# Attention's output transposed by DMA and normalised on GpSimd, in a kernel that runs top-k attention and a Fourier mix

## The chip, the cores and the metric

The kernel runs on one core of one Trainium2 chip. A core has a matrix engine (TensorE, PE in the profile, its weight loads PEld), a vector engine (VectorE, DVE), a scalar engine (ScalarE, ACT), a general engine (GpSimd, POOL) and a synchronisation engine (SyncE, SP) that here issues nearly all DMA transfers. Each engine works through its own instructions in order and waits on semaphores for the others. The metric is the device time of one execution in microseconds (us).

## The reference, cut to what matters

```python
# attention: batch 8, heads 8, tokens 576, head size 64
scores = scale * q @ k.T
kth = np.partition(scores, -32, axis=-1)[..., -32:-31]
scores = np.where(scores >= kth, scores, -1e9)
attn = softmax(scores)                       # sum + 1e-9
x = (attn @ v) laid out as [batch, token, 8 * 64]

# Fourier mix: d_model 512, hidden 2048
mixed = real(fft(fft(x, axis=1), axis=2))
u = x + mixed
un = (u - mean(u)) / sqrt(var(u) + 1e-6)
out = u + relu(un @ w_ch1) @ w_ch2
```

All of it is in 32-bit floats. The inputs are q, k and v of shape [8, 8, 576, 64] and the two weight matrices.

## The kernel before

**Tiles and steps.** Two heads make a pair, so there are 32 pairs, four for each batch. The 576 queries of a pair are cut into tiles: eight tiles of 128 queries of one head, and one tile with the 64 remaining queries of both heads. That is nine tiles a pair (IN_PAIR, PER_PAIR), 36 a batch, 288 in all. One main loop (L1485) runs over steps i, one step for each tile, and goes on behind the last tile until all planned work is done. A step issues work of several tiles: the scores of tile i+3 on PE, the top-32 search of tile i on DVE (four MAX8 and three MATCH_REPLACE8 over 576 scores, `top_ops`, L422 and L424), the bounds of tile i on POOL (`bounds`, L431), the mask of tile i-1 (ACT L443, POOL L446) and its exponentials (ACT L454).

**From the exponentials to the attention's output.** In pairs 4 to 30 without pair 7 (`by_dma`, L435) the exponentials reach TensorE over DRAM. One step after the exponentials, `plane` has ACT copy their 16-bit low and high halves into two planes (L467), and SP write them to DRAM (L480, L483). One step later, `turn` has SP bring them back with a DMA transpose (L501) into PT, with keys on the partitions. In the other pairs TensorE transposes them (`transposes`). A pair's queries form two chunks: chunk 0 has 320 queries and chunk 1 has 256 (CW). `attend` multiplies PT by v for one chunk, 20 matmuls in the profile (L559), into the PSUM tile o, which has one buffer (ps_o). `chunk_at` says in which step this happens: the fourth after the chunk's last tile in the pairs with DMA, as the last of the step's matmuls.

**From the output to tokens.** `attended` (L568) follows at once in the same step: ACT copies o to SBUF as xT (L573), copies two denominators (L578) and adds 1e-9 to the denominators (L585); DVE takes the reciprocals one step later (L586). Then the chunk is put in the list pending, for the next step or later. `to_tokens` (L589) takes it from there, one chunk a step at most: TensorE transposes xT in three or two pieces into PSUM (tpx, L599), and DVE multiplies by the reciprocals into x (L603, L610). In batch 1 ACT does this multiplication instead, in pieces of one head (L622). x holds all tokens of a batch and has two buffers. A chunk of batch b therefore waits in pending until the output of batch b-2 has been put out (`written`).

**The Fourier mix.** When a batch's four pairs are in x, its later stages are planned in steps counted from T0 (L1377), which is end + 5 for batches 2 to 6, where end is the step of the batch's last tile. The stages are: folds on POOL (`fold_tails`, `fold_ops`), the token DFT (`dft_tokens`, PE L750), the channel DFT (`dft_channels`, PE L807 and L811), statistics on DVE, an inverse square root on DVE and POOL, and transposes to channels first (PE L876). Then the MLP of the batch is cut into units (`mlp_units`) that enter a queue: 32 units with the hidden layer (PE L961, ACT L965), then units with the second layer (PE L988, L1027, and for one chunk a form with seven half-size products, PE L1158, with sums on POOL L1103 and L1130 and with parts of w2 that SP loads, L904). `level` (L1458) sets how much PE work a step should have, so that the queue is empty when the next batch's units arrive; `fixed_cost` (L1447) is its estimate of what a step has in any case. Units are put between the fixed pieces of a step. Work behind the last tile, the stages and MLP of the last batch, has no attention beside it.

**Order around the change.** In each step the order of issue is: `turn`, mask and `plane`; the scores of a new tile and their ACT copies; the list planned for "act" and the list out_next; then the other pieces with units between them; then `attend` and `attended`; the loads of q, k and v (SP, L240 to L288); the DVE search; the list planned for "pool0"; the bounds; and the lists "dve", "pool", "load" and "load2".

Of the kernel before, what the change touches and what calls it, by code (L numbers as in the profile page):

```python
# [73 lines left out]
def kernel(  # L74
# [359 lines left out]

    def by_dma(i):  # L435

        pair = i // PER_PAIR
        return NPB <= pair < NPAIR - 1 and pair != 2 * NPB - 1
# [129 lines left out]
    def attended(pair, ch, late):  # L568

        o, w = o_of.pop((pair, ch)), CW[ch]  # L570
        PT.pop((pair, ch))
        xT = attp.tile([P, CW[0]], F32, name=f"xT_{pair}_{ch}", tag="xT", bufs=4)
        nc.scalar.copy(out=xT[:, 0:w], in_=o[:, 0:w])  # L573
        xT_of[pair, ch] = xT
        den = den_t[pair % 3]
        if ch == 0:
            for h in range(2):
                nc.scalar.copy(  # L578
                    out=den[TH * h:TH * (h + 1), 5:6],
                    in_=den[TAIL + TH * h:TAIL + TH * (h + 1), 4:5],  # L580
                )
        c0, n = (0, 6) if ch == 0 else (6, 4)
        rd = small.tile([P, 6], F32, name=f"rd_{pair}_{ch}", tag="rd", bufs=6)

        nc.scalar.activation(out=rd[:, 0:n], in_=den[:, c0:c0 + n], func=AF.Copy, bias=1e-9)  # L585
        late.append(lambda: nc.vector.reciprocal(out=rd[:, 0:n], in_=rd[:, 0:n]))  # L586
        rd_of[pair, ch] = rd

    def to_tokens(pair, ch, at_once=True):  # L589
# [5 lines left out]
        xT, rd = xT_of.pop((pair, ch)), rd_of.pop((pair, ch))  # L595
        shape, name = [P, 4, P], f"tpx_{pair}_{ch}"
# [3 lines left out]
        cols = slice(P * hp, P * (hp + 1))  # L600
# [772 lines left out]
    for b in range(B):  # L1373
# [3 lines left out]
        T0 = end + (2 if first else 3 if soon else 4 if last else 5)  # L1377
# [69 lines left out]
    def fixed_cost(i):  # L1447
# [5 lines left out]
        t += 0.0 if ch is None else (CW[ch] / 115.0 + 0.14 * len(CHUNKS[ch]))  # L1453
# [31 lines left out]
    while i < N + 5 or plan or queue or sums:  # L1485
# [117 lines left out]
        for where in ("pool", "pool2", "load", "load2"):  # L1603
            run(i, where)
# [40 lines left out]
```

## Time and profile before

| | |
|---|---|
| time, three runs | median 1886.04 us (1885.32 to 1888.74) |
| the profiled execution's own time | 1888.63 us |
| its span, first to last instruction | 1886.8 us |
| granted TensorE clock, mean | 0.954 of full speed |
| busy, share of the span | PE 1724.3 us (91%), DVE 1582.2 (84%), ACT 1295.8 (69%), POOL 912.1 (48%) |
| DMA | 249 MB, 51% of the 16 DMA engines' time |

The profile is of one execution. Engines' busy times leave out waiting and the issuing of DMAs. A line number such as L573 is a line of the kernel before. A group of instructions is written as line, engine, operation, output<-inputs with shapes, and count, and then busy time, the mean duration of one in nanoseconds, and the idle time of the engine just before them with what ended it. The matmuls overlap in the pipeline, so that the mean duration of one is longer than the distance from one to the next. A wait "ACT xT L573 <- PE o L559" says that ACT stood idle before the instruction of line 573 until the matmul of line 559 was done. SPq lines are instructions of SyncE's queue.

### The profile page before, as it was taken

Reading aid. Unit: us, or ns where it says so; the run is one execution under the profiler, and the core shown is the slowest. Engines: PE = TensorE matmul, PEld = TensorE weight load, DVE = VectorE, ACT = ScalarE, POOL = GpSimd, SP = SyncE. Lnnn points to the kernel's source line nnn. Section 1 sums busy time; section 2 is a strip of 40 time slices with the busy share of each in tenths; the row PEclk is TensorE's granted clock in tenths of the full one; section 3 lists DMA queues with packets and bytes.
Section 4 is the critical chain, followed back from the end, with each engine's and each line's share of the span. In section 5 each row is a group of like instructions: output and inputs, shape, how many; then the busy total and the mean of one; then the engine's idle time right before and its main releaser. Section 6 shows DMA issues by size and latency. Waiting matters only on the chain.

```text
span 1886.8 us, 26907 instructions
## 1 busy us (share of the span) xinstructions
PE 1724.3 (91%) x8134; PEld 1089.6 (58%) x8134; DVE 1582.2 (84%) x3301; ACT 1295.8 (69%) x3104; POOL 912.1 (48%) x1278
## 2 busy tenths in 40 slices
PE   6667699889899999999999999999999999999999
PEld 3344365355456654566456665566556655667677
DVE  7999999799899999997998898999999899862110
ACT  6878658577787777776777677777787678652100
POOL 4768644454745366354643465355544464341012
PEclk8778899899899999999999999999999999999999
DMA  5333026661557755575465845586467655440132
GB/s 166 103 97 108 20 63 160 166 156 32 137 149 193 186 130 137 140 202 140 122 157 136 225 121 128 142 220 156 120 160 179 179 132 144 120 117 6 51 110 72
DMA packets 516576, 249.16 MB, mean 132 GB/s; under 512 B 398288, under 2 KB 506448, under 8 KB 516432
## 3 DMA queue, kind: packets, MB, share of 16 engines
q1 hardware_dynamic: 515664, 247.23, 50.6%
q8 instruction: 65, 1.06, 0.2%
q14 instruction: 79, 0.65, 0.1%
q10 hardware_dynamic: 768, 0.21, 0.0%
HBM read 93.63 MB, written 84.74 MB: 95 GB/s over the span
## 4 chain that ended last, share of the span: by engine, by line
PE 63%; DVE 12%; ACT 10%; POOL 6%; DMA 4%; issue 3%; SPq 2%; POOLq 0%; DVEq 0%; ACTq 0%
PE hp L961 23%; PE cp L988 8%; PE o L559 7%; DVE m L422 5%; PE sp L398 5%; DVE wk L424 5%; PE cw L1158 3%; PE yp L750 3%; PE cv L1158 3%; PE cp L1027 2%; POOL wk L446 2%; ACT wk L443 2%; ACT wk L467 2%; PE sp_t L368 2%; PE mp L811 1%
## 5 line engine op out<-in xcount | busy, mean ns | idle before, releaser
L446 POOL TENSOR_TENSOR wk<-S,wk 128x576 f32<-128x576 f32 x288 | 408.6, 1419 | 572.2 <-ACT wk L443 570.0
L422 DVE MAX8 m<-wk 128x8 f32<-128x576 f32 x864 | 626.4, 749 | 6.0
L961 PE MATMUL hp<-unT,w 128*128 128x256 f32 (+1 forms) x2048 | 535.5, 412 | 3.6 <-ACT hT L965 2.8
L961 PEld LDWEIGHTS hp<-unT,w 128*128 128x128 f32 x2048 | 378.5, 191 | 134.5 <-issue 30.1
L424 DVE MATCH_REPLACE8 wk<-m,wk 128x576 f32<-128x576 f32 x576 | 427.4, 742 | 0.0
L467 ACT COPY wk<-S 128x576 uint16<-128x576 uint16 x468 | 288.7, 666 | 0.1
L443 ACT ACTIVATE wk<-S,nt 128x576 f32<-128x576 f32 x288 | 222.2, 772 | 73.0 <-POOL nt L431 72.1
L988 PE MATMUL cp<-w,hT 128*128 128x512 f32 x512 | 244.6, 614 | 0.0
L422 DVE MAX8 m<-S 128x8 f32<-128x576 f32 x288 | 213.9, 743 | 31.9 <-ACT S L372 31.8
L559 PE MATMUL o<-PT,v 128*64 128x256 f32 (+3 forms) x1440 | 205.1, 429 | 19.3 <-DMA PT<-planes 15.4
L424 DVE MATCH_REPLACE8 wk<-m,S 128x576 f32<-128x576 f32 x288 | 213.5, 741 | 0.0
L965 ACT ACTIVATE hT<-hp 128x320 f32<-128x320 f32 (+1 forms) x256 | 103.6, 409 | 155.3 <-PE hp L961 154.5
L454 ACT ACTIVATE S<-wk,nt 128x576 f32<-128x576 f32 x234 | 182.6, 781 | 39.9 <-POOL wk L446 38.9
L398 PE MATMUL sp<-kT,qT 64*128 64x512 f32 (+1 forms) x528 | 183.1, 693 | 12.2 <-ACT means L1346 5.1
L559 PEld LDWEIGHTS o<-PT,v 128*64 128x64 f32 x1440 | 118.0, 158 | 105.0 <-issue 35.5
L988 PEld LDWEIGHTS cp<-w,hT 128*128 128x128 f32 x512 | 93.4, 195 | 109.5 <-issue 107.7
L401 ACT COPY S<-sp 128x512 f32<-128x512 f32 (+1 forms) x264 | 141.6, 586 | 18.5 <-PE sp L398 17.6
L1103 POOL TENSOR_TENSOR hT<-hT 128x512 f32<-128x512 f32 x64 | 81.3, 1274 | 99.0 <-ACT hT L965 86.2
L368 PEld LDWEIGHTS sp_t<-kt,qT 128*128 128x128 f32 x320 | 55.7, 198 | 100.6 <-ACT S L390 44.2
L368 PE MATMUL sp_t<-kt,qT 128*128 128x128 f32 x320 | 72.1, 308 | 45.0 <-ACT S L390 29.8
L431 POOL TENSOR_TENSOR nt<-m,cc 128x2 f32<-128x2 f32 x288 | 58.9, 205 | 111.9 <-DVE m L422 108.9
L1158 PE MATMUL cw<-w,hT 128*128 128x256 f32 x448 | 105.7, 383 | 0.7 <-issue 0.6
(160 smaller groups left out, 2137.9 us busy)
## 6 DMA issues: line engine op xcount, KB each, us to landing
planes<-wk SPq DMA_DIRECT2D x208, 288.0 KB, 2.7
w<-w_parts SPq DMA_DIRECT2D x82, 512.0 KB, 4.7
space<-in_moe_w_ch_dram SPq DMA_DIRECT2D x32, 512.0 KB, 3.7
nat<-in_q_dram SPq DMA_DIRECT2D x128, 64.0 KB, 2.4
v<-in_v_dram SPq DMA_DIRECT2D x64, 128.0 KB, 3.0
out_dram<-x SPq DMA_DIRECT2D x32, 256.0 KB, 2.6
nat<-in_k_dram SPq DMA_DIRECT2D x62, 128.0 KB, 2.9
planes<-wk SPq DMA_DIRECT2D x52, 144.0 KB, 2.6
```

Source lines behind the costliest of these rows:

```text
L368: nc.tensor.matmul(sp[:, 0:P], lhsT=qT[:, q_end - P:q_end], rhs=kt_t, start=True, stop=True)
L398: nc.tensor.matmul(sp[r], lhsT=qT[hd, q_cols], rhs=kT[hd, :], start=True, stop=True)
L422: ops.append(lambda src=src, m8=m8: nc.vector.max(out=m8, in_=src))
L424: ops.append(lambda src=src, m8=m8: nc.vector.match_replace(w, m8, src, NEG))
L443: nc.scalar.activation(out=w, in_=Ssb[i], func=AF.Relu, scale=-FAR, bias=Nt[i][:, 1:2])
L446: nc.gpsimd.tensor_tensor(out=w, in0=Ssb[i], in1=w, op=ALU.subtract)
L454: nc.scalar.activation(out=Ssb[i] if by_dma(i) else w, in_=w, func=AF.Exp, bias=Nt.pop(i)[:, 0:1], accum_out=den_t[pair % 3][:, c:c + 1],)
L467: nc.scalar.copy(out=words[:, half, :], in_=src[:, half, :])
L559: nc.tensor.matmul(o[D * e:D * (e + 1), c0:c1], lhsT=vv[:, c, e, :], rhs=pt[:, NF if c == NF else (NF + 1) * e + c, c0:c1], start=(c == 0) ...
L961: nc.tensor.matmul(hp[:, 0:w], lhsT=w1[:, dt, P * it:P * (it + 1)], rhs=unT[:, dt, 0:w], start=(dt == 0), stop=(dt == NDT - 1),)
L988: nc.tensor.matmul(cp, lhsT=hT[:, it, P * n:P * (n + 1)], rhs=w2[:, it, :], start=(it == 0), stop=(it == NIT - 1),)
L1158: nc.tensor.matmul(dst, lhsT=h()[a][:, kc, :], rhs=rhs_of(kc), start=start and kc == 0, stop=kc == NK - 1, skip_group_check=True,)
```

## The change

In the pairs 4 to 30 without 7 (now `pair_by_dma`) a chunk's output goes to x without TensorE and DVE:

- ACT copies o twice, as 16-bit low and high halves, into two planes in SBUF, instead of once in 32 bits.
- SP writes the planes to DRAM (one write for chunk 1, two for chunk 0), and `to_tokens` has SP bring them back with DMA transposes straight into x (one for chunk 1, two for chunk 0), at the end of the step in which the chunk is taken from pending.
- POOL multiplies x in place by the reciprocals two steps later, in the list "pool0", ahead of the step's bounds (one instruction for chunk 1, two for chunk 0).
- `attended` is put in out_next for all of these chunks but the last of each batch: its ACT copies then stand in the next step, behind the copies of the scores. The chunk can be taken from pending from the step after that on, also in a step that has a chunk's `attend`.
- T0 of batches 2 to 6 is two steps later, end + 7, and the loop's end and `fixed_cost` follow.

```diff
         o, w = o_of.pop((pair, ch)), CW[ch]
         PT.pop((pair, ch))
-        xT = attp.tile([P, CW[0]], F32, name=f"xT_{pair}_{ch}", tag="xT", bufs=4)
-        nc.scalar.copy(out=xT[:, 0:w], in_=o[:, 0:w])
-        xT_of[pair, ch] = xT
+        if pair_by_dma(pair):
+            words = attp.tile([P, 2, CW[0]], U16, name=f"ow_{pair}_{ch}", tag="xT", bufs=4)
+            src = o[:, 0:w].bitcast(U16).rearrange("p (s h) -> p h s", h=2)
+            for half in range(2):
+                nc.scalar.copy(out=words[:, half, 0:w], in_=src[:, half, :])
+            to = xT_of[pair, ch] = dramp.tile(
+                [P, 2, CW[0]], U16, name=f"oplanes_{pair}_{ch}", tag="oplanes", bufs=6
+            )
+            nc.sync.dma_start(out=to[:, :, TAIL:], in_=words[:, :, 0:2 * P])
+            if ch == 0:
+                nc.sync.dma_start(out=to[:, :, 0:TAIL], in_=words[:, :, 2 * P:])
+        else:
+            xT = attp.tile([P, CW[0]], F32, name=f"xT_{pair}_{ch}", tag="xT", bufs=4)
+            nc.scalar.copy(out=xT[:, 0:w], in_=o[:, 0:w])
+            xT_of[pair, ch] = xT
...
         xT, rd = xT_of.pop((pair, ch)), rd_of.pop((pair, ch))
+        cols = slice(P * hp, P * (hp + 1))
+        if pair_by_dma(pair):
+            rows = xT.rearrange("p h s -> (p h) s")
+            nc.sync.dma_start_transpose(
+                out=x[:, 2 * ch:2 * ch + 2, cols].bitcast(U16), in_=rows[:, TAIL:]
+            )
+            if ch == 0:
+                nc.sync.dma_start_transpose(out=x[:, 4:5, cols].bitcast(U16), in_=rows[:, 0:P])
+
+            def normalise_in_place():
+                for t0, nt, n, r in ((2 * ch, 2, 0, P), (4, 1, 4, TAIL))[:2 - ch]:
+                    xs = x[0:r, t0:t0 + nt, cols].rearrange("p t (e d) -> p t e d", e=2)
+                    by = rd[0:r, n:n + 2 * nt].rearrange("p (t e) -> p t e", e=2)
+                    nc.gpsimd.tensor_tensor(
+                        out=xs, in0=xs, in1=by.to_broadcast([r, nt, 2, D]), op=ALU.mult
+                    )
+
+            at(now[0] + 2, "pool0", normalise_in_place)
+            return 0.0
...
-        T0 = end + (2 if first else 3 if soon else 4 if last else 5)
+        T0 = end + (2 if first else 3 if soon else 4 if last else 7)
...
         if pending and pending[0][0] <= i and (
-            i < 2 * PER_BATCH + 4 or chunk_at(i)[0] is None
+            i < 2 * PER_BATCH + 4 or chunk_at(i)[0] is None or pair_by_dma(pending[0][1])
         ):
             _, pp, pc = pending[0]
             if pp // NPB < 2 or pp // NPB - 2 in written:
                 pending.pop(0)
-                tok.append(lambda: to_tokens(pp, pc, not short))
+                if not pair_by_dma(pp):
+                    tok.append(lambda: to_tokens(pp, pc, not short))
+                else:
+                    at(i, "turn", lambda: to_tokens(pp, pc))
...
             cost += attend(pair, ch)
-            attended(pair, ch, late_next)
-            pending.append((i + 1, pair, ch))
+            if pair_by_dma(pair) and (pair % NPB, ch) != (NPB - 1, 1):
+                out_next.append(lambda pair=pair, ch=ch: attended(pair, ch, late_next))
+                pending.append((i + 2, pair, ch))
+            else:
+                attended(pair, ch, late_next)
+                pending.append((i + 1, pair, ch))
...
-        for where in ("pool", "pool2", "load", "load2"):
+        for where in ("pool", "pool2", "load", "load2", "turn"):
             run(i, where)
```

More of the change, by code (lines that the diff above doesn't have):

```diff
@@ L433, in bounds, with pair_by_dma @@
             )
+    def pair_by_dma(pair):
+        return NPB <= pair < NPAIR - 1 and pair != 2 * NPB - 1
     def by_dma(i):
-        pair = i // PER_PAIR
-        return NPB <= pair < NPAIR - 1 and pair != 2 * NPB - 1
+        return pair_by_dma(i // PER_PAIR)
     def mask(i, then=None):
@@ L599, in to_tokens @@
             nc.tensor.transpose(tp[0:ROWS[t], n, :], xT[:, P * n:P * n + ROWS[t]], ident)
-        cols = slice(P * hp, P * (hp + 1))
         def normalise():
@@ L1452, in fixed_cost @@
         ch = chunk_at(i)[1] if i > PER_BATCH + 3 else {4: 0, 8: 1}.get((i - 3) % PER_PAIR)
-        t += 0.0 if ch is None else (CW[ch] / 115.0 + 0.14 * len(CHUNKS[ch]))
+        t += 0.0 if ch is None else (
+            CW[ch] / 115.0 + (0.0 if by_dma(i - 4) else 0.14 * len(CHUNKS[ch]))
+        )
         if i < N and i % PER_PAIR in (0, 5):
@@ L1484 @@
     i, carry = 0, 0.0
-    while i < N + 5 or plan or queue or sums:
+    while i < N + 7 or plan or queue or sums:
         now[0] = i
```

## The prediction

> **What bounds the kernel now.** I read the busy shares first, by stage. Each line is a stretch of the run: us, then busy time and instruction count of PE, PEld, DVE, ACT and POOL, the granted TensorE clock, the DMA share and GB/s.
>
> ```profile
> 450.00:860.00 410.00, 377.09 (x1759) 230.12 (x1757) 379.82 (x789) 307.33 (x728) 207.09 (x307) 0.95 0.61 153
> 860.00:1640.00 780.00, 756.32 (x3638) 473.88 (x3637) 717.93 (x1494) 594.74 (x1420) 393.41 (x591) 0.98 0.60 151
> 1640.00:1887.00 247.00, 241.92 (x1129) 177.80 (x1127) 70.98 (x155) 60.41 (x147) 56.17 (x80) 1.00 0.24 74
> ```
>
> From 860 us on TensorE sets the pace (97% busy, VectorE 92%); behind 1640 it works almost alone. Between 450 and 860 the two are level (92% and 93%), so whichever is late holds the other. The next view is the chain that ended last, in order of time; a line is start, duration, what.
>
> ```profile
> 1000.05 0.22 PE tpx L599 x2
> 1000.27 2.16 PE hp L961 x8
> ...
> 1004.80 0.33 PE tpx L599 x3
> ...
> 1052.89 2.48 DMA planes<-wk
> ...
> 1055.43 5.20 DMA PT<-planes
> ```
>
> The reader is to see two things. The output's transposes (tpx) lie on the chain, but each costs only 0.11 us there, since matmuls overlap. And the chain does pass through the DMA route of the probabilities, one write and one transpose, 7.7 us in a row. Then the waits: who waited for whom, total us, times, longest; the last two lines are SyncE's own waits.
>
> ```profile
> POOL wk L446 <- ACT wk L443: 570.0, 247, 14.7
> ...
> ACT xT L573 <- PE o L559: 86.3, 38, 11.8
> ...
> DVE x L603 <- PE tpx L599: 47.3, 18, 6.6
> ...
> PE sp_t L368 <- ACT S L390: 29.8, 21, 3.6
> ...
> PE o L559 <- DMA PT<-planes: 15.4, 6, 7.4
> ```
> ```profile
> SPq L480 <- ACT wk L467: 374.7, 133, 16.9
> SPq L501 <- DMA planes<-wk: 202.9, 107, 4.1
> ```
>
> GpSimd has hundreds of idle microseconds. ScalarE stands still for o at 38 of 64 chunks, and TensorE for probabilities only at 6. Last, the prices: groups by shape (count, busy us, mean ns, idle before), and the duration of SyncE's transposes (min/median/max ns).
>
> ```profile
> L603 DVE TENSOR_TENSOR x<-tpx,rd 128x256 f32<-128x256 f32 x57 | 24.0, 421 | 53.9 <-PE tpx L599 47.3 <-DMA nat<-in_q_dram 3.0 <-issue 1.4
> L610 DVE TENSOR_TENSOR x<-tpx,rd 64x128 f32<-64x128 f32 x28 | 7.6, 273 | 0.0
> L573 ACT COPY xT<-o 128x320 f32<-128x320 f32 x32 | 13.7, 427 | 51.1 <-PE o L559 51.1
> L573 ACT COPY xT<-o 128x256 f32<-128x256 f32 x32 | 11.9, 371 | 35.4 <-PE o L559 35.2
> L918 POOL TENSOR_TENSOR w_t<-w 128x256 f32<-128x256 f32 x16 | 11.7, 731 | 34.8 <-DMA w_parts<-w_t 34.8
> ```
> ```profile
> L501 SPq DMA_TRANSPOSE PT<-planes x130: 1293/2504/7872, 254.6 to 1651.1; - x130
> ```
>
> **The change, part by part.** The sum is made against the profiled execution, 1888.6 us (span 1886.8). That is 2.6 above the median of 1886.0, which I take off at the end. Affected are pairs 4 to 30 without 7: 26 pairs, 52 chunks.
>
> *TensorE's transposes go.* Five a pair, 130 of 160. At the 0.11 us of the chain that is 0.55 a pair, 14.3 in all (the 280 ns of their row would make 36, but that row counts the overlapped latency). Pairs 16 to 30 lie in the stretch that TensorE bounds: 15 x 0.55 = 8.2, all of it on the path. The other 11 pairs hold 6.0; VectorE is level there, so I take half. -11.2, ends -14.3 and -4. What is late next is VectorE, 5 points behind.
>
> *VectorE's normalise goes.* 22 pairs (4 to 6 do it on ScalarE) by 2 x 421 + 273 ns = 1.1 us, 24.5 in all, and waits of 47.3 for tpx. From 860 on VectorE has cover from TensorE, so there I count nothing; without that cover the 15 pairs are worth 16.7. For pairs 8 to 15 the work is 8.9 and the waits in that window 9.7. Ends 0 and -18.6, I take a third: -6.
>
> *ScalarE's copies.* Two 16-bit copies per chunk take the place of one of 32 bits. No row shows a 16-bit copy out of PSUM. Below, it costs what the 32-bit copy of as many elements does (427 and 371): +0.8 us a pair, +21. Above, 666 ns each, the row of the 576-element 16-bit copies (L467): 2.66 for 0.80, +48. I take the lower, which has the same element count and source. Pairs 4 to 6 lose ten ScalarE multiplies of about 0.32 each (L622), -9.6. Net +11 of busy time on an engine that is 69% busy: +2 on the path, ends -9.6 and +38.
>
> *The wait for o goes.* L573 stood at the end of the step of its matmuls, and behind it in ScalarE's queue were the denominators, the next step's mask and planes, and the scores' copies. Now 47 of the 52 stand behind the scores' copies of the next step, which come after o on TensorE anyway. ScalarE still waits for TensorE there, but mask and planes are done by then. TensorE itself is hurt by a late ScalarE where sp_t waits for a free bank: 29.8 on L390 above, and 14.8 on L401 in the same view. I take a sixth of the 44.6, since most of it belongs to steps without a chunk: -7. Ends -30 (two thirds of it), and +10 if the copies, now ahead of exp and of the q and k copies, delay those by 0.4 us at 26 places.
>
> *The later stages of batches 2 to 6 move two steps back.* With T0 move the folds (GpSimd), both DFT stages, their ScalarE copies, statistics and rsqrt, the MLP's units, and what these put on SyncE's queue: the loads of w2's parts and the output stores. One batch has 535.5 + 244.6 + 64.7 + 209.5 (L961, L988, L1027, L1158) = 1054/8 = 132 us of MLP on TensorE, 3.7 a step of 36. Two steps' worth, 7.3, moves out of the time that VectorE shares into the time behind the last scores. Batch 1's MLP is thinned over two steps more, which gives a part back. +5, ends 0 and +11.6 (two whole steps; 15 pairs of nine steps in 780 us make 52 a pair, 5.8 a step).
>
> *GpSimd's normalise comes.* Per pair two of 128x256 and one of 64x128, by L918 and the 465 ns of the 128x128 rows: 1.9 us, 50 in all. It stands two steps behind the transpose's issue, before the bounds (L431); behind those wait ScalarE's mask, then L446, then exp. Cover: 570 us of idle time before L446, and the two vector instructions, 1.5 us, that follow a tile's last MAX8 in its step. +1, ends 0 and +10; a gain is excluded, since it only adds.
>
> [...]
>
> *SyncE and the DMAs.* 78 writes and 78 transposes more, in a queue of 650 to 800 instructions. A write's issue took 0.56 (L480). No row has a transpose this small: 131 KB for two blocks of tokens, 66 KB for the tails, against 590 KB in 2.50 us. By size 0.56 and 0.28 us of issue; above, 1.29 each, the shortest seen. So 2.8 to 5.6 us of SyncE in a pair's 52. The write waits for ScalarE's copies; behind it stand the loads of k, v and q. The transposes wait for that write, once a batch also for the output store of batch b-2, and behind them stands the next PT<-planes, for which TensorE's o matmuls wait. SyncE's 375 us of waiting for ScalarE are the cover. +5, ends 0 and +30.
>
> Sum: -11.2 - 6 + 2 - 7 + 5 + 1 + 5 = -11.2. 1888.6 - 11.2 = 1877.4, less 2.6: 1875.
>
> **The rivals.**
> *Slower: the probabilities queue behind the output.* Place: SyncE, where the x transposes stand just ahead of the next PT<-planes. For it: the chain runs through that route already (1052.89 to 1060.6), and SyncE took up to 7.9 us for one transpose. Against it: 46 of 52 chunks had no such wait. Price: 0.6 to 2.6 us at each chunk that has no slack; at 14 of 52 and 2 us it is 28 in place of my 5: 1898. It decides from about 8 chunks on (16 us in place of 5 cancels the gain).
> *Given back at the end.* The two steps cost their full 11.6, and VectorE's part hides behind ScalarE and GpSimd between 290 and 860: -11.2 + 2 - 7 + 11.6 + 1 + 5 = +1.4, 1887. For it: TensorE has 242 of 247 us behind 1640, so nothing there absorbs more. Against it: batch 1 gets the two steps.
> *More than that.* ScalarE's 86 us of waiting for o is what makes sp_t late: -30 in place of -7, 1852. For it: 35 sp_t waits in the two rows, 1.3 us each. Against it: L390's step comes once a pair, not next to a chunk's.
> That the change does not do what it says is excluded by its order: 130 fewer transposes, 78 more on SyncE.
>
> **How the numbers follow.** About 0.2% (3.8 us) is what this measurement can tell from no change. Forecast 0.46, slower rival 0.28, given back 0.15, more 0.11. Faster: 0.40 of the forecast's, all of the third and a little of the second, 0.53. Slower: 0.26 of the first rival, 0.07 of the second, 0.03 of the forecast's, 0.36. The rest, 0.11, is within. Range: from the third rival, 1852, to the first with the shift's upper end, 1898 + 6, and 3 of ScalarE: 1907. The forecast's own range is 1865 to 1884.
>
> **What would show it.** Right: tpx rows 30 in place of 160, ScalarE's wait for o under 20 us, VectorE's wait for tpx under 15; TensorE above 96% from 860 on; sp_t's waits for L390 below 24. SyncE's x transposes at 0.3 to 1.3 us. Wrong: o's wait for PT<-planes above 30 us, bounds or L446 waiting for x transposes, last scores later than before, or more than 255 us behind them.

## The result and the profile after

The change makes the kernel slower: median 1900.4 us (1897.6 to 1903.2, four runs) against 1886.9, a ratio of 1.0068 with a 95% interval of 1.0053 to 1.0084, or +13.5 us. The prediction was 1875, a gain; its stated range, 1852 to 1907, holds the measured time near its slow end.

The busy shares by stage of the changed kernel (columns as before the change):

```profile
450.00:860.00 410.00, 370.86 (x1722) 224.98 (x1718) 381.50 (x783) 315.00 (x751) 217.69 (x321) 0.96 0.68 167
860.00:1640.00 780.00, 735.28 (x3485) 458.06 (x3483) 694.98 (x1421) 590.35 (x1413) 407.71 (x622) 0.98 0.65 160
1640.00:1902.00 262.00, 255.11 (x1184) 186.08 (x1182) 70.50 (x155) 65.57 (x163) 62.44 (x90) 1.00 0.26 76
```

TensorE, which set the pace from 860 to 1640 us, now stands idle for 780 - 735.3 = 44.7 us there; before it was 780 - 756.3 = 23.7. Its clock in that stretch is the same. Behind 1640 it has 13 us more to do.

The waits say for what it stands (who, for whom: total us, times, longest):

```profile
DVE m L422 <- ACT S L372: 81.6, 31, 7.8
...
PE sp_t L368 <- ACT S L401: 22.8, 15, 6.3
...
PE o L561 <- DMA PT<-planes: 19.1, 11, 6.1
...
PE cw L1190 <- DMA w<-w_parts: 15.9, 6, 5.1
PE sp_t L368 <- ACT S L390: 15.1, 15, 2.7
...
PE cp L1059 <- DMA w<-w_parts: 13.1, 6, 3.2
...
POOL x L623 <- DMA x<-oplanes: 12.8, 12, 2.1
...
DVE x L635 <- PE tpx L632: 6.5, 3, 3.2
...
ACT ow L578 <- PE o L561: 2.1, 2, 1.3
```

What the change was to remove is gone: ScalarE's wait for o fell from 86.3 to 2.1 (and 9.3 where the old path stays), VectorE's wait for tpx from 47.3 to 6.5. VectorE's search now waits longer for the copied scores (81.6 for 31.8). What is new stands in a place that the prediction did not price: TensorE waits 15.9 + 13.1 = 29.0 us for `w<-w_parts`, the loads of w2's parts between the seven products of the later stages. In the kernel before, the only such row of TensorE's matmuls was this:

```profile
PE cp L1027 <- DMA w<-w_parts: 6.0, 2, 5.5
```

From 860 us on, in the stretch where TensorE is idle for 21.0 us more, the kernel before has no such row, and the changed kernel has these two, 17.5 us together:

```profile
PE cw L1190 <- DMA w<-w_parts: 10.5, 3, 3.6
...
PE cp L1059 <- DMA w<-w_parts: 7.0, 3, 2.7
```

One of these waits in the chain of the changed kernel that ended last (start, us, what):

```profile
1035.71 2.49 SPq L503
...
1038.31 0.57 SPq L485
...
1038.93 0.60 SPq L485
...
1039.62 4.42 DMA w<-w_parts
1044.05 0.14 issue
1044.18 5.39 PE cw L1190 x16
```

The load stands in SyncE's queue behind a transpose of the probabilities (2.49) and two writes of their planes (0.57 and 0.60); ahead of these SyncE issued one of the change's own transposes (L613, 1.21 us from 1034.46). The load then takes 4.42 us, and TensorE starts 0.14 us after it has landed. TensorE had stood still for 3.3 us.

Where the 14.5 us between the two profiled spans lie can be read from the start of the bounds of a pair's first tile. Up to pair 16 the changed kernel gains 13.9 (861.3 to 847.4 us). From pair 16 to pair 31 it takes 796.4 in place of 778.9, +17.5. From pair 31 to the end it takes 257.5 in place of 246.7, +10.8. Such a split compares single executions. It also compares schedules: an edit that moves stages changes which units the planner puts into which step.

### The profile page after: what moved, and what is told of

It reads as the page before. It is cut to its first block, busy times and chain, and to the rows that moved or that the text cites. A ratio compares the mean times of both kernels' runs of the same rounds, so it can differ in the third digit from the quotient of the medians.

```text
span 1901.3 us, 26874 instructions
## 1 busy us (share of the span) xinstructions
PE 1705.1 (90%) x8004; PEld 1073.9 (56%) x8004; DVE 1564.7 (82%) x3232; ACT 1304.7 (69%) x3126; POOL 951.0 (50%) x1356
## 4 chain that ended last, share of the span: by engine, by line
PE 55%; DVE 13%; POOL 9%; DMA 8%; ACT 8%; SPq 3%; issue 3%; POOLq 0%; DVEq 0%; ACTq 0%
PE hp L993 18%; PE cp L1020 8%; PE o L561 6%; DVE m L422 6%; DVE wk L424 5%; PE sp L398 4%; PE cw L1190 4%; PE cv L1190 3%; DMA w<-w_parts 3%; POOL wk L448 3%; PE yp L782 3%; PE cp L1059 3%; DMA PT<-planes 2%; ACT wk L445 2%; DMA planes<-wk 2%
## 5 line engine op out<-in xcount | busy, mean ns | idle before, releaser
L422 DVE MAX8 m<-S 128x8 f32<-128x576 f32 x288 | 214.6, 745 | 84.5 <-ACT S L372 81.6
L445 ACT ACTIVATE wk<-S,nt 128x576 f32<-128x576 f32 x288 | 222.4, 772 | 77.2 <-POOL nt L431 76.8
L1020 PE MATMUL cp<-w,hT 128*128 128x512 f32 x512 | 238.0, 604 | 0.0
L561 PE MATMUL o<-PT,v 128*64 128x256 f32 (+3 forms) x1440 | 201.9, 425 | 23.9 <-DMA PT<-planes 19.1
L398 PE MATMUL sp<-kT,qT 64*128 64x512 f32 (+1 forms) x528 | 172.2, 674 | 15.8 <-ACT means L1378 5.1
L1190 PE MATMUL cw<-w,hT 128*128 128x256 f32 x448 | 112.9, 401 | 18.0 <-DMA w<-w_parts 15.9
L1190 PEld LDWEIGHTS cw<-w,hT 128*128 128x128 f32 x448 | 86.8, 200 | 36.4 <-issue 20.7
```

The source lines that it names most:

```text
L398: nc.tensor.matmul(sp[r], lhsT=qT[hd, q_cols], rhs=kT[hd, :], start=True, stop=True)
L422: ops.append(lambda src=src, m8=m8: nc.vector.max(out=m8, in_=src))
L445: nc.scalar.activation(out=w, in_=Ssb[i], func=AF.Relu, scale=-FAR, bias=Nt[i][:, 1:2])
L561: nc.tensor.matmul(o[D * e:D * (e + 1), c0:c1], lhsT=vv[:, c, e, :], rhs=pt[:, NF if c == NF else (NF + 1) * e + c, c0:c1], start=(c == 0) ...
L1020: nc.tensor.matmul(cp, lhsT=hT[:, it, P * n:P * (n + 1)], rhs=w2[:, it, :], start=(it == 0), stop=(it == NIT - 1),)
L1190: nc.tensor.matmul(dst, lhsT=h()[a][:, kc, :], rhs=rhs_of(kc), start=start and kc == 0, stop=kc == NK - 1, skip_group_check=True,)
```

## The experiments

Medians of each kernel beside runs of the kernel before on the same chip; the ratio is to those, with its 95% interval.

### The two parts that need no DMA

The shift of the later stages alone, in the kernel before:

```diff
-        T0 = end + (2 if first else 3 if soon else 4 if last else 5)
+        T0 = end + (2 if first else 3 if soon else 4 if last else 7)
```

> The kernel before, with only the later stages of batches 2 to 6 two steps back (end + 7). Theory S (the new writes and transposes fill SyncE's queue, and TensorE waits behind them for parts of w2 and for probabilities): about what the prediction had for this part, +5, 1887 to 1893, and no wait of TensorE for w<-w_parts above 2 us in all from 860 us on. Rival T (the two steps back are the loss, because the MLP's loads now meet the attention's in the wrong steps): 1898 or more, with such waits.

Measured 1901.3, ratio 1.0071 (1.0043 to 1.0099). The shift alone costs about as much as the whole change, 14.4 us by the medians and 8 to 19 by the interval, and it brings the waits that rival T named. Its profiled execution is the fastest of its four and 8.9 us longer than the one before: up to pair 16 it gains 9.2, from there to pair 31 it loses 9.9, and behind pair 31's start 8.2. TensorE's matmuls wait 15.3 us for w2's parts in place of 6.0.

The later place of ScalarE's copies alone, in the kernel before:

```diff
-            attended(pair, ch, late_next)
-            pending.append((i + 1, pair, ch))
+            dma_pair = NPB <= pair < NPAIR - 1 and pair != 2 * NPB - 1
+            if dma_pair and (pair % NPB, ch) != (NPB - 1, 1):
+                out_next.append(lambda pair=pair, ch=ch: attended(pair, ch, late_next))
+                pending.append((i + 2, pair, ch))
+            else:
+                attended(pair, ch, late_next)
+                pending.append((i + 1, pair, ch))
```

> The kernel before, with only ScalarE's copies of o (still one of 32 bits) moved into the next step behind the scores' copies. Theory S with the prediction's sizes: 7 less, 1876 to 1883, ScalarE's wait for o under 15 us in place of 86. Rival: the 15 us by which the changed kernel is ahead at pair 18 come from VectorE and TensorE, freed of the transposes, and this part alone gives nothing, 1884 to 1889.

Measured 1885.0, ratio 0.9993 (0.9974 to 1.0011): no difference. ScalarE's wait for o, 86.3 us before, is 10.8 in this kernel, and the time is the same. By the pairs' starts its profile gains 15.7 us up to pair 16, as much as the changed kernel, and loses 8.9 and 2.8 behind it. So this early gain also comes where TensorE's transposes and VectorE's normalise stay.

### The output's DMAs

The changed kernel without them; x is multiplied from a constant table, so the output's way to x is left out. Then the same with the 78 writes put back.

```diff
-            nc.sync.dma_start(out=to[:, :, TAIL:], in_=words[:, :, 0:2 * P])
...
-            nc.sync.dma_start_transpose(
...
-                        out=xs, in0=xs, in1=by.to_broadcast([r, nt, 2, D]), op=ALU.mult
+                        out=xs, in0=fd[0:r, 0:nt, :].rearrange("p t (e d) -> p t e d", e=2), in1=by.to_broadcast([r, nt, 2, D]), op=ALU.mult
```

> The changed kernel without the writes and transposes of the output: x is multiplied from a table instead, so the later stages work on other numbers; all else stays, the two steps back, the 16-bit copies and GpSimd's multiply. Theory S: the loss goes, 1868 to 1880. Rivals (the two steps back, ScalarE's second copy, GpSimd's multiply ahead of the bounds): 1893 to 1900.

> The same, but the 78 writes of the output to DRAM stay and only the 78 transposes are left out. SyncE's time for them is 49 us of writes and 103 of transposes. Theory S, by SyncE's time: about a third of what the run without both gains is lost again, 1875 to 1886. If the waits of the transposes count (for the write's landing, for x), and not the time they take, this run is as fast as the one without both.

Measured 1872.0 (0.992, 0.9895 to 0.9946) without any, and 1890.2 (1.0013, 0.9995 to 1.0031) with the writes. The first lies in the range of theory S, with both steps of the shift still in place. The second lies above its range: in this schedule the writes make 18 us and the transposes 10 more. TensorE's waits for w2's parts are 20.5, 30.4 and 29.0 us in the three kernels, those for the probabilities (PE and PEld) 15.5, 20.2 and 27.9.

Three ways to make the same DMAs cheaper followed: the writes at the end of the step, the writes issued by ScalarE, and the transposes behind the probabilities' transpose of the next step.

```diff
+            at(now[0], "turn", write)
```

> The changed kernel with the output's writes put at the end of their step in SyncE's order, behind the loads of w2's parts, of k, q and v, in place of right behind ScalarE's copies. The same 78 writes and transposes. Theory wait (the writes cost 18 us because SyncE stands still for ScalarE's copies in the middle of the step, and the loads behind it with it): 10 to 18 less than the changed kernel, 1882 to 1890. Rival time (what counts is the 0.57 us that each write takes of SyncE): unchanged, 1897 to 1903.

```diff
-            nc.sync.dma_start(out=to[:, :, TAIL:], in_=words[:, :, 0:2 * P])
+            nc.scalar.dma_start(out=to[:, :, TAIL:], in_=words[:, :, 0:2 * P])
```

> The changed kernel with the output's writes issued by ScalarE behind its own copies, in place of SyncE. Theory wait and theory time both: SyncE is rid of them, and 12 to 18 us go, 1882 to 1890, if ScalarE's 78 issues of about 0.5 us are hidden. If the DMA engines' load, not SyncE, is what counts: unchanged, 1897 to 1903.

```diff
-            at(now[0] + 2, "pool0", normalise_in_place)
+            at(now[0] + 1, "pool0", normalise_in_place)
...
-                    at(i, "turn", lambda: to_tokens(pp, pc))
+                    at(i + 1, "turned", lambda pp=pp, pc=pc: to_tokens(pp, pc))
...
+        run(i, "turned")
```

> The changed kernel with the output's transposes one place later in SyncE's order, behind the next step's transpose of probabilities in place of ahead of it. Theory order (the loss by the transposes, 10 us, is the probabilities' queueing behind them): 5 to 10 less, 1890 to 1896, and TensorE's wait for PT<-planes back to about 16 us. Theory time: unchanged, 1897 to 1903.

Measured 1905.0 (1.0103, 1.0077 to 1.013), 1914.4 (1.0146, 1.0127 to 1.0165) and 1917.5 (1.0173, 1.014 to 1.0205). None is faster than the changed kernel (the first is 5 us slower, little more than the noise), so the gains that the theories of waiting, time and order expected did not come. The last two edits bring a cost of their own, so they do not exclude that SyncE's time or the order has a part. In the second, ScalarE stands still for 53.0 us at its 78 issues: 36.6 ahead of the denominators' copies and 16.4 ahead of the addition of 1e-9, two waits that the changed kernel does not have. In the third, GpSimd's multiply stays in its step with its input a step later, and its wait grew to this (the changed kernel: 12.8). TensorE's wait for the probabilities grew there too, from 19.1 to 24.5, though their transposes now went first:

```profile
POOL x L623 <- DMA x<-oplanes: 39.2, 25, 4.8
```

The writes with their bytes cut to a sixteenth (no transposes, x from the constant table):

```diff
-            nc.sync.dma_start(out=to[:, :, TAIL:], in_=words[:, :, 0:2 * P])
+            nc.sync.dma_start(out=to[0:8, :, TAIL:], in_=words[0:8, :, 0:2 * P])
```

> The kernel with the 78 writes and without the transposes (x is multiplied from a constant table, the output's way to x is left out), with each write cut from 128 partitions to 8: the same number of issues on SyncE, in the same places with the same waits, a sixteenth of the bytes and descriptors. With full writes it took 1890.2, without any 1872.0. Theory 'bytes' (the DMA engines' load delays the probabilities and the weights): 1873 to 1877. Theory 'issue' (SyncE's instructions and what they wait for cost, whatever they carry): 1887 to 1892. Between the two, both take part, in that proportion.

Measured 1893.4 (1.0024, 1.0011 to 1.0038): as slow as with all bytes. The bytes are not the cause of the writes' 18 us.

### The shift, again

One step in place of two, with GpSimd's multiply one step behind the transposes:

```diff
-            at(now[0] + 2, "pool0", normalise_in_place)
+            at(now[0] + 1, "pool0", normalise_in_place)
...
-        T0 = end + (2 if first else 3 if soon else 4 if last else 7)
+        T0 = end + (2 if first else 3 if soon else 4 if last else 6)
```

> The changed kernel with GpSimd's multiply one step behind the transposes in place of two, which lets the later stages of batches 2 to 6 begin at end + 6, one step back in place of two. Theory shift (two steps back cost 8 to 10 us of TensorE's work behind the last scores): half of it goes, 3 to 6 less, 1894 to 1898, the stretch behind pair 31's first bounds 252 to 254 us in place of 257.5. If GpSimd now waits for the transposes and holds back the bounds: 1900 to 1910.

Measured 1932.0 (1.0243, 1.0218 to 1.0269), 32 us slower than the changed kernel and outside both ranges. The multiply now waits, and behind it wait the bounds, then ScalarE's mask (76.8 in the changed kernel). The later stages moved too, so how much of the 32 is the multiply's is not shown:

```profile
ACT wk L445 <- POOL nt L431: 116.4, 68, 6.9
POOL x L623 <- DMA x<-oplanes: 58.0, 26, 7.7
```

No output DMAs and no shift (x from the constant table, T0 at end + 5, the multiply at once):

```diff
-            at(now[0] + 2, "pool0", normalise_in_place)
+            normalise_in_place()
...
-        T0 = end + (2 if first else 3 if soon else 4 if last else 7)
+        T0 = end + (2 if first else 3 if soon else 4 if last else 5)
```

> The kernel without the output's DMAs (x is multiplied from a constant table, so that the output's way to x is left out and the result is not the reference's), but with the later stages of batches 2 to 6 where they stood before the change (five steps behind the batch's end), and the multiply at once. Theory A (the parts add): the shift alone cost 14.4 us, the DMAs 28.4, so what the change removes, net of what it adds on ScalarE and GpSimd, is worth 1900.4 - 28.4 - 14.4 - 1886.9 = -29; expected 1857.6, within 5. Theory B (the shift costs only in a schedule that is already tight, and is hidden where the output's work is gone): as with the shift, 1872, within 4; the removed work is then worth only 15.

Measured 1900.8 (1.0063, 1.0045 to 1.0081). Both theories miss, by 43 and 29 us: taking the shift out of the kernel of 1872 made it 29 slower, where putting the shift into the kernel before made that 14 slower. Prices for the parts do not add. The multiply's new place shows no cost in the waits: GpSimd waits 1.9 us before it, and the mask's wait for the bounds is 75.9 (75.5 in the kernel of 1872). Here too TensorE waits for w2's parts (20.8 us), now in three waits of 4.4 to 5.3 us between 1050 and 1480 us. Around one of them the windows of 4 us of that kernel show what such a wait brings besides itself (the number behind POOL's is the granted clock):

```profile
1260.00:1264.00 4.00, 0.00 (x0) 0.00 (x0) 3.96 (x9) 2.55 (x5) 1.56 (x2) 0.91 1.04 294
1264.00:1268.00 4.00, 3.70 (x11) 1.68 (x13) 0.77 (x2) 0.00 (x0) 0.00 (x0) 0.50 0.82 224
1268.00:1272.00 4.00, 4.00 (x19) 2.02 (x16) 0.00 (x0) 0.00 (x0) 0.00 (x0) 0.74 0.82 190
```

TensorE runs no matmul for 4 us, and then at half its clock for over 4 us. The half clock makes this kernel lose more than its waits say. Over the two halves of the stretch from 860 us, first this kernel, then the one of 1872:

```profile
860.00:1250.00 390.00, 373.28 (x1767) 234.00 (x1766) 353.16 (x725) 302.51 (x724) 211.72 (x321) 0.97 0.59 150
1250.00:1640.00 390.00, 368.41 (x1712) 227.23 (x1711) 339.36 (x695) 288.15 (x688) 195.10 (x305) 0.96 0.58 146
```
```profile
860.00:1250.00 390.00, 374.67 (x1776) 236.35 (x1775) 356.27 (x729) 303.36 (x728) 212.30 (x321) 0.98 0.61 155
1250.00:1640.00 390.00, 373.29 (x1799) 233.45 (x1798) 354.14 (x724) 296.77 (x711) 204.12 (x314) 1.00 0.59 147
```

The lost clock, 0.01 and 0.04 of 390 us, is worth about 4 and 16 us by estimate.

The last pair of each batch by TensorE and VectorE as before, so that the shift can be undone in a kernel with the whole result; and the same with one write a chunk:

```diff
+    def out_by_dma(pair):
+        return pair_by_dma(pair) and pair % NPB != NPB - 1
...
-        T0 = end + (2 if first else 3 if soon else 4 if last else 7)
+        T0 = end + (2 if first else 3 if soon else 4 if last else 5)
...
```

> The changed kernel, but the last pair of each batch (11, 15, 19, 23, 27) keeps TensorE's transposes and the vector engine's normalise, so that the later stages stand five steps behind the batch's end, as before the change. 21 of 26 pairs go by DMA. Theory A (the parts add): the shift's 14.4 goes, 21/26 of -29 and of +28.4 stay: 1886.9 - 23.4 + 22.9 = 1886.4, within 5. Theory C (the shift costs nothing beside the DMAs, since the last tiles then wait for the probabilities anyway): 1898 to 1901.

```diff
-            for half in range(2):
-                nc.scalar.copy(out=words[:, half, 0:w], in_=src[:, half, :])
+            nc.scalar.copy(out=words[:, :, off:off + 2 * P], in_=src[:, :, 0:2 * P])
+            if ch == 0:
+                nc.scalar.copy(out=words[:, :, 0:TAIL], in_=src[:, :, 2 * P:])
...
-            nc.sync.dma_start(out=to[:, :, TAIL:], in_=words[:, :, 0:2 * P])
-            if ch == 0:
-                nc.sync.dma_start(out=to[:, :, 0:TAIL], in_=words[:, :, 2 * P:])
+            c0 = 0 if ch == 0 else TAIL
+            nc.sync.dma_start(out=to[:, :, c0:], in_=words[:, :, c0:])
```

> As the kernel in which the last pair of each batch goes by TensorE, but with ScalarE's copies arranged so that one write a chunk carries all of it: 42 writes in place of 63, the same bytes; ScalarE has one copy less at the second chunk. Theory 'issue' (SyncE's instructions cost, 18.2 us for 78 writes, 0.23 each): 5 us below that kernel, about 1881. Theory 'bytes': as that kernel, within 2, less a little for ScalarE (21 fixed costs of some 0.2 us, hidden).

Measured 1918.1 (1.0153, 1.0134 to 1.0172) and 1913.7 (1.0134, 1.0117 to 1.0152). Both theories of the first miss: undoing the shift in this way, with 5 of 26 pairs back on TensorE, made the changed kernel 18 slower. A third of the writes less points to a small gain, but the two intervals overlap. (The fixed cost of 0.2 us in the second expectation is an estimate: the changed kernel's 444 ns for 320 columns and 395 for 256 leave about 0.2 us at none.)

The kernel before with its later stages one step later:

```diff
-        T0 = end + (2 if first else 3 if soon else 4 if last else 5)
+        T0 = end + (2 if first else 3 if soon else 4 if last else 6)
```

> The kernel before with its later stages of batches 2 to 6 one step later (six behind the batch's end in place of five; seven cost 14.4). Theory 'steady price' (each step moved costs its work at the end of the run and in the stretch before): 1894, 1891 to 1897. Theory 'place' (what costs is where in a pair's nine steps the loads of w2's parts and their products fall): the change of the time is 4 for the work at the end plus the change in TensorE's waits for these loads, and may have either sign.

Measured 1912.3 (1.012, 1.0092 to 1.0149): one step costs 24, two cost 14. A steady price per step is excluded. The 'place' theory's formula does not give the size either: 4 plus 13.1 more of waits for w2's parts is 17. TensorE also stands still for other reasons there: four times 2.9 us before the transposes to channels first (L876), and each time half clock follows. From 860 to 1640 us the half clock lasts 51.2 us in place of 27.3, worth about 12 by estimate.

### The loads of w2's parts

Both kernels without these loads in batches 1 to 6 (the products multiply wrong blocks of w2):

```diff
+            load = bring if last else lambda *what: None
...
-                bring(T2, w2_12, part)
+                load(T2, w2_12, part)
...
```

> The changed kernel without the loads of w2's parts in batches 1 to 6 (the seven products then multiply by the wrong blocks of w2, the result is not the reference's; the arithmetic and its order stay). To be read against the kernel before with the same left out. Theory 'loads' (the loss is TensorE waiting for these loads, 29.0 us in this kernel against 6.0 before): 23 goes from the difference of +13.5, so this kernel is 9.5 below the other, -5 to -14; by itself about 1871. Theory 'elsewhere' (these waits stand in for others that would come in their place, such as those for the probabilities, for free score banks or at the end of the run): the difference stays, +8 to +14.

> The kernel before without the loads of w2's parts in batches 1 to 6 (wrong blocks of w2, as above). Both theories: its waits for these loads are 6.0 us, so 1879 to 1887, less if the bytes of these loads hold up other transfers.

Measured 1855.4 (0.9817, 0.9794 to 0.984) for the changed kernel and 1868.7 (0.9888, 0.9863 to 0.9912) for the kernel before. With the loads the change loses 13.5; without them it gains 13.4. The change of sign is what the theory 'loads' expected and the other excludes, at the lower end of its range. By itself each kernel is faster than expected (1871 and 1879 to 1887). The stages of the changed kernel without the loads, then of the kernel before without them:

```profile
450.00:860.00 410.00, 381.39 (x1807) 233.17 (x1808) 395.04 (x812) 329.12 (x784) 226.47 (x339) 0.97 0.58 140
860.00:1590.00 730.00, 702.58 (x3397) 440.75 (x3396) 679.32 (x1391) 577.10 (x1382) 401.04 (x613) 1.00 0.58 141
1590.00:1853.00 263.00, 257.77 (x1197) 188.36 (x1196) 74.47 (x163) 68.53 (x170) 63.73 (x92) 1.00 0.19 58
```
```profile
450.00:860.00 410.00, 379.24 (x1811) 233.08 (x1810) 386.70 (x804) 316.17 (x749) 211.18 (x313) 0.97 0.51 127
860.00:1590.00 730.00, 712.21 (x3462) 447.21 (x3461) 689.93 (x1435) 566.04 (x1348) 382.29 (x577) 0.99 0.52 128
1590.00:1864.00 274.00, 270.05 (x1257) 196.86 (x1255) 92.18 (x204) 80.89 (x197) 64.50 (x89) 1.00 0.19 59
```

By the pairs' starts, the change then gains 15.8 up to pair 16 and 6.3 from pair 16 to 31, and pays 10.7 behind pair 31's start. So the early gain and the price at the end are there with and without the loads; the loads turn the middle from -6.3 into +17.5. They cost more than the waits put down to them: taking them away saves 45 us in the changed kernel, where TensorE's waits for them are 29.0, and 19 in the kernel before, where they are 6.0. In the changed kernel two other things shrink with them: the half clock from 860 to 1640 us from 30.7 to 6.8 us (worth about 12 by estimate), and the waits for the probabilities (PE and PEld) from 27.9 to 21.5. The loads' waits, their place in SyncE's queue and their bytes go together here, so these runs show that the loss hangs on the loads, and not by which of the three.

The last two of the seven products swapped, in the changed kernel:

```diff
-                for f in (p2, p1, p5, p4, p6, p3, p7) for part in range(2)
+                for f in (p2, p1, p5, p4, p6, p7, p3) for part in range(2)
```

> The changed kernel with the last two of the seven products swapped, so that two units of other work stand between the last load of a part of w2 and the tails' product that reads it (L1059). Theory 'loads': the 13.1 us of TensorE waiting at L1059 go, and 1887 to 1890 results, if the load before the product that is now earlier (T3, for the seventh product) still comes in time; one product of slack less, so it may give back up to as much in waits at L1190. Theory 'elsewhere': 1898 to 1902.

Measured 1908.1 (1.0094, 1.0067 to 1.0122). Of the 13.1 us at the tails' product 7.8 stay, and the products wait 17.4 in place of 15.9. The expected 10 to 13 us do not come, and the kernel is rather slower (by 8, but the intervals overlap): part of a product's slack was moved from one load to another.

Eight products that need no loads, in batches 1 to 6; first in the changed kernel, then with the shift undone as above:

```diff
-            seven = b and ch == 0 or last
+            seven = last
...
-            if b and not last:
-                need((b, 0, "x", 4))
```

> The changed kernel, where batches 1 to 6 multiply their first chunk by w2 with eight products that read w2 as it lies, in place of seven that need its parts loaded. By columns, 32 matmuls of 512 in place of 56 of 256, 2048 columns more a batch: two of the planner's units of 1.75 us, 3.5 a batch, 21 in all; GpSimd loses 48 sums of 1.27 us. Theory 'loads': the time without these loads, 1855.4, plus 21: 1876, 1868 to 1884, so faster than both kernels. Theory 'stand-in' (the loads only filled time that something else takes as soon as TensorE has its full work): 1890 to 1905.

> The same with the last pair of each batch by TensorE and the later stages five steps behind the batch's end. Theory 'loads': without loads whose place matters, the shift costs only its work at the end, 10.7 us (255.5 against 244.8 behind pair 31's start in the two kernels without these loads); 5 of 26 pairs lose the gain of 22 before that, 4: 1876 - 10.7 + 4 = 1869, 1861 to 1878. Theory 'place' (also without these loads the time depends on the step at which the later stages fall, through the probabilities' and the output's own transfers): outside that, 1880 or more.

Measured 1862.2 (0.986, 0.9825 to 0.9895) and 1872.8 (0.9922, 0.9898 to 0.9946). The first is faster than its range and beats both kernels: 26 us below the runs of the kernel before beside it (1888.5) and 38 below the changed one, although TensorE has more columns to multiply. Its stretch from 860 on:

```profile
860.00:1640.00 780.00, 765.32 (x3445) 444.43 (x3444) 718.04 (x1465) 605.68 (x1444) 383.83 (x606) 0.99 0.55 137
```

TensorE is idle for 14.7 us there, in place of 44.7. The second lies in the range expected, but not for the reason given: the part behind pair 31's start falls by 11.4 as expected (257.5 to 246.1), yet pair 31 starts 20.5 later (1624.8 against 1604.3). So a step's place matters also without these loads, by less. In all three schedules that hold the rest of the change, undoing the shift made the kernel slower (1872.0 to 1900.8, 1900.4 to 1918.1, 1862.2 to 1872.8); only in the kernel before is the shift itself a loss. The kernel before with eight products was not run; from its time without the loads, 1868.7, and the 6.8 by which eight products exceed leaving the loads out in the changed kernel, an estimate is 1875.5. By that about half of the 26 would be the change's and half the products'.

## Why the prediction was wrong, point by point

- **The step that failed: the loads of w2's parts, which the sum put at nothing.** The prediction named them among what goes along with "the later stages move two steps back" (+5 between 0 and +11.6), but priced only TensorE work there; in "SyncE and the DMAs" (+5) they are not among what stands behind the writes. No term is for TensorE waiting for them. The runs showed that the loss hangs on them: with the loads the change costs 13.5 us, without them in both kernels it gains 13.4. TensorE's waits for them are 29.0 us in place of 6.0. That it is the loads' place against SyncE's transposes and writes is seen at single waits of the chain and argued from the shift, not shown for the whole.
- **The shift itself.** Its work was sized well: 10.8 us behind pair 31's start, near the upper end. By itself the shift costs 14.4 (8 to 19) and a shift by one step 24, so a price per step moved is wrong. But it is not the step that makes the changed kernel lose, since undoing it there made the kernel slower each time.
- **The nearness of 13.4 to the sum's 11.2 is in part luck.** The gain up to pair 16 (15.8 without the loads) is larger than the terms for it, the gain behind it (6.3) and the price at the end (10.7) differ as well, and the wait for o gave nothing.
- **"SyncE and the DMAs", +5 between 0 and +30.** In the changed schedule it is 28 (1872.0 to 1900.4), at the upper end, and so by size the term that was furthest off. (Its lower bound of SyncE's time for a pair, 2.8, adds up to 3.1 from its own prices.) The transposes took the upper bound of their duration whatever their size, 131 or 66 KB (ns, min/median/max):

```profile
L613 SPq DMA_TRANSPOSE x<-oplanes x52: 1192/1252/3037, 296.4 to 1681.2; - x52
L617 SPq DMA_TRANSPOSE x<-oplanes x26: 1186/1232/2142, 297.8 to 1662.2; - x26
```

  The 28 is not the price of these DMAs alone: with all of them and without w2's loads the changed kernel is the faster of the two. It is the price of both together; that they meet in SyncE's queue is seen at single places of the chain, not shown for all of it.
- **"The wait for o goes", -7.** The wait went, the gain was 0: the run with this part alone lies 1.4 us below the kernel before, and its interval includes zero. TensorE's 44.6 us for score banks became 37.9 in the changed kernel, and 43.1 with the later copies alone.
- **TensorE's transposes and VectorE's normalise, -11.2 and -6.** They are gone as said (30 transposes of 160 stay). The early stretch gained 13.9, and 15.8 without w2's loads, where I had 3 of TensorE's and VectorE's 6 and some of the rest. That it is theirs is not shown: ScalarE's later copies alone start pair 16 15.7 us earlier, and the shift alone 9.2. From pair 16 on, 6.3 is left without the loads, which holds all of the change's parts in that stretch; the 8.2 put there is not measured by itself. (VectorE's part counts 22 pairs; pairs 8 to 30 are 23, and no term of the sum hangs on it.)
- **ScalarE's copies, +2.** The lower price was right: 444 and 395 ns, against 427 and 371 for the 32-bit copies.

```profile
L578 ACT COPY ow<-o 128x320 uint16<-128x320 uint16 x52 | 19.9, 444 | 0.0
...
L578 ACT COPY ow<-o 128x256 uint16<-128x256 uint16 x52 | 17.2, 395 | 2.1 <-PE o L561 2.1
```

- **GpSimd's normalise, +1.** It took 31.8 + 10.2 = 42 us of work in place of 50; the multiply of 128x256 took 611 ns on GpSimd (L623 of the changed kernel) where VectorE's had taken 421 (L603 before). These 42 us did not appear in full in the time, since the whole change gains 13.4 without w2's loads, and the mask's wait for the bounds rose only from 72.1 to 76.8. No run has the multiply by itself. With the multiply one step earlier, GpSimd's wait for its input was 58.0 and the mask's 116.4.
- **The rivals.** The slower rival's number, 1898, was near, its mechanism was not: TensorE's waits for the probabilities grew by 3.7 us (11.2 with those of its weight loads), and the transposes behind the probabilities made it worse. "Given back at the end" was right in its own part (10.8 of its 11.6), and far too small.
- **The signs.** That TensorE would be above 96% busy from 860 on (94%), that the last scores would not be later than before (3.6 us later) and that at most 255 us would follow them (257.5) told against the forecast; both of the latter are read from the start of pair 31. So did GpSimd's waits for x transposes ahead of the bounds (12.8). The signs for it came as well: 30 tpx rows, ScalarE's waits for o of 11.4, VectorE's for tpx of 6.5, those for L390 of 15.1, x transposes of 1.2 us. They show that the old waits went, and not that the time followed. The sign for the slower rival, o waiting over 30 us, was not reached.

What stays open: why the output's 78 writes make 18 us when their bytes, their place in the step and their issue by ScalarE do not explain it (10 of it are TensorE's waits for w2's parts, shown in the waits but not by an experiment of their own); and what sets the time of a given step's place beyond these waits, since the formula for one step missed by 7.

## What to carry to other kernels

When a change moves a stage of a tuned schedule, list each load that the stage issues between two of its own products, with the time from the end of the product before to the start of the product behind and what SyncE issues in between; the queue position of such a load is a term of the sum, and a price per step moved is not. A wait of TensorE of 2 us and more is charged with the half clock that followed 79 of 99 such stretches here, while a long wait of an engine that TensorE does not wait for may be worth nothing, as the 86 us for o were. A form with fewer multiplications can be the slower one when it needs operands loaded in the middle of its chain, as the seven products were here by 38 us.

## What the runs showed of the hardware

**The clock behind a wait.** In the traces of the 18 experiments, from 860 to 1600 us, the granted clock was either 1.0 or 0.5, and the half clock came in pieces of 3.41 us (multiples of it where pieces join); in the kernel before it came, from 860 to 1640 us, four times for 3.41 us and twice for 6.83, in the changed one seven times for 3.41 and once for 6.83. A stretch without a matmul counts here as followed by half clock if a piece begins between its start and 1.5 us behind its end. Of 159 stretches of 0.7 to 2.0 us 6 were followed by it; of 99 stretches of 2.0 us and more 79 were, 27 of 35 already at 2.0 to 2.5 us. In the kernel before and the changed one together it followed 1 of 19 of 0.7 to 2.0 us and 10 of 11 of 2.0 us and more. By these numbers a piece can cost an estimated 1.7 us, half of its 3.41, on top of the wait. In the changed kernel around 1044 us:

```profile
1040.00:1044.00 4.00, 0.84 (x4) 0.39 (x3) 3.96 (x9) 1.20 (x3) 1.77 (x3) 1.00 0.94 265
1044.00:1048.00 4.00, 3.82 (x12) 3.22 (x13) 3.93 (x9) 0.00 (x0) 0.00 (x0) 0.69 1.19 290
1048.00:1052.00 4.00, 4.00 (x21) 2.00 (x22) 3.12 (x6) 2.40 (x5) 1.19 (x1) 0.88 1.09 361
```

From 860 to 1640 us the half clock lasted 27.3 us in the kernel before and 30.7 in the changed one, so by estimate it is at most about 2 us of the 13.5, half of the 3.4 between them; it was 51.2 us in the kernel with neither DMAs nor shift and 20.5 in the one of 1872.

**Transposes by DMA.** For 66 and 131 KB alike the issue took 1.2 us of SyncE (medians 1.23 and 1.25), for 590 KB 2.45 us: between the two smaller sizes half the bytes saved next to nothing.

**Seven against eight products.** With the loads out of the way on both sides, in the changed kernel eight products with matmuls of 512 columns took only 6.8 us more in all than seven with matmuls of 256, where the planner's price for the columns makes it 21. The two intervals overlap, and the eight also leave out 48 sums of GpSimd, so this is the whole kernel's difference and not TensorE's price.
